# One scaling, two stores and a few pieces of bookkeeping change their steps at the end of the attention, before an MoE

## The chip, the core and the metric

The kernel runs on one core of a Trainium2 chip. A core has a matmul engine (TensorE, PE in the profile) and three engines for elementwise work: VectorE (DVE), ScalarE (ACT) and GpSimd (POOL). SyncE (SP) issues transfers between the chip's memory (HBM) and on-chip memory (SBUF); POOL issues the indirect ones. Matmuls write to PSUM, which DVE and ACT read. Each engine works off its instructions in the order of the program and waits for the others through semaphores. The metric is the time of one execution on the device, in microseconds.

## The reference

The inputs are q, k, v of shape (8, 12, 448, 64) in float32 (8 batches, 12 heads, 448 positions) and the weights of a mixture of 8 experts.

```
scores = cap * tanh(q @ k^T / 8 / cap)            # cap 30
attn   = softmax(scores)                          # over the keys
x      = (attn @ v) as rows of 768, 3584 tokens   # 12 heads side by side
e      = argmax(x @ w_gate);  g = softmax(x @ w_gate)[e]
out    = g * (relu(x @ w1[e]) @ w2[e])            # w1: 768x1024, w2: 1024x768
```

## The kernel before

**Attention.** The 12 heads of a batch are 6 pairs, so there are 48 pairs and a loop of 49 steps, n = 0 to 48. Step n computes the scores of pair n (`scores`, PE, then tanh and exp on ACT), the sums of exponentials of pair n in two additions on DVE and a third for the short last 64 keys (`adds`; POOL does the third, except for the last pair, where DVE does it), and the product with v of pair n - 1 (`pv`, PE), whose result DVE copies to a tile `ot`. `turn` transposes on DVE the `ot` of pair n - 2 into a tile `yt` that collects a batch.

**What follows a batch.** When batch b is through (step n = 6b + 6), a chain of small pieces is spread over the next steps: `rec_v`, `rec_p`, `rec_c` (reciprocals of the sums, DVE, PE, DVE), `logits` (PE, into PSUM tile ps_l), `log_v` (DVE, writes `lr`), `log_p` (PE, ps_l again), `route_v` (DVE), `route_s` (ACT), `place_p` (PE), `route_g` (DVE), `place_v` (DVE: reads ps_l and counts tokens of each expert), `scale` (DVE: two halves of `yt`, 128 x 1344 each, times gate and reciprocal), `store` (SP: four transfers of `yt` into `xd` in HBM, each of 32 partitions of both halves) and `place_d` (POOL: the tokens' numbers scattered to their slots in `ids`).

**Order.** The whole program is ordered by hand; each engine gets its instructions in the order in which the code below emits them. Pieces are put at a step and at one of six places in it by `at(step, place, function, ...)` (line 1033), and within a place they run in the order of the calls. Step n emits: `turn(n - 2)`; place 0; `scores(n)`, first half; `pv(n - 1)`, first half; place 5; `adds(n, 0)`; `scores(n)`, second half; place 3; `pv(n - 1)`, second half, with the copy to `ot`; place 6; `adds(n, 1)`; place 1; place 2. Step 48 has no scores: it begins with `adds(47, 1)`, and goes on with place 0, `pv(47)`, places 5, 3, 6, 1 and 2.

For batch 6 (the seventh) `log_v` stands in step 45, `place_p`, the second scaling and the first two stores in step 47, the last two stores in step 48. Batch 7's first `logits` stand in step 48, place 5.

**The first blocks of the experts.** Tokens are worked off in blocks of at most 448 of one expert. Block -1 is chosen after batch 4 and its rows are gathered from `xd` into `xg` during batches 5 and 6. Each of its 6 parts (128 of the 768 columns) is then transposed by DVE (`trans_x`, into one of three tiles `xt`), rounded by ACT to a high part (`high_x`) and subtracted by DVE to a low part (`low_x`); products use high and low parts of both factors, three matmuls for one. Block -2 is chosen by `first_block(1)`, 20 small DVE instructions in a row that `decide(k)` issues in pieces of k steps.

**After step 48** comes block -1: `up(-1, f)` (PE: 18 matmuls into one of two tiles ph; ACT: Relu to the high part of the hidden rows; DVE: the low part), and among it the pieces of batch 7 and the splits of weights into high and low. Behind `up(-1, 0)` stand on PE the last sums and `logits` of batch 7, `up(-1, 1)`, `rec_p(7)` and `up(-1, 2)`; on DVE, behind the low part of `up(-1, 0)`, stands `rec_v(7)`; on SP, behind the stores of step 48, the row of block -2's expert (`first_row`) and the loads of its weights (`load_w0`). The hidden rows of the first three f lie in `h0`, a tile that takes the name and the pool of the tiles `yt`, of which there are two buffers, given out in turn; batches 0, 2 and 4 use other memory:

```
 345               yts[b] = yp.tile([128, QB, XW], F32, name="yt", bufs=2)
 943       hb = h0 if j == -1 and f < 3 else m["hb"]
 945       A.activation(out=hh, in_=ph, func=AF.Relu)
 946       V.scalar_tensor_tensor(out=hl, in0=ph, scalar=0.0, in1=hh, op0=ALU.max, op1=ALU.subtract)
1147       h0 = yp.tile([128, QB, XW], F32, name="yt", bufs=2).rearrange("p q x -> p (q x)").bitcast(F32R)
1148       up(-1, 0)
1162       first_row(1)
1163       for f in range(2):
1164           load_w0(-2, f)
1165       rec_v(b)
```

Of the kernel before, what the change touches and what calls it, by code (L numbers as in the profile page):

```python
# [15 lines left out]
B, H, S, D = 8, 12, 448, 64  # L16
# [110 lines left out]
def attention_moe(tc, qT, kT, vL, capd, wgL, w1a, w1b, w2a, w2b, cst, cmk, out):  # L127
    nc = tc.nc
    V, A, G, PE = nc.vector, nc.scalar, nc.gpsimd, nc.tensor
# [903 lines left out]
    def at(step, when, f, *a):  # L1033
        tasks.setdefault((step, when), []).append((f, a))
# [5 lines left out]
    for b in range(B):  # L1040

        n = b * NP + NP
        for g in range(1, NP, 2):
            i = b * NP + g
            at(i + 2, 5, sums, i)
        at(n, 5, logits, b, range(4))
        at(n + 1, 3 if b == B - 1 else 5, logits, b, range(4, NP))
        if b == B - 1:
            break
        at(n + 1, 6, rec_v, b)  # L1050
        at(n + 2, 3, rec_p, b)
        at(n + 2, 6, rec_c, b)
        at(n + 3, 0, log_v, b)
        at(n + 3, 6, log_p, b)
        at(n + 3, 1, route_v, b)
        at(n + 4, 5, route_s, b)
        at(n + 5, 5, place_p, b)
        at(n + 4, 6, route_g, b)
        at(n + 4, 1, scale, b, 0, V)
        at(n + 5, 0, scale, b, 1, V)  # L1060
        at(n + 5, 2, store, b, range(0, 2))
        at(n + 5, 6, place_v, b)
        at(n + 6, 2, store, b, range(2, 4))
        if b < B - 2:
            for q in range(4):

                at(n + (5 if b == B_FIRST[0] - 1 else 11 if b == 4 else 7), 2, place_d, b, q)
# [11 lines left out]
        g += w  # L1079


    for n, k, late in ((8, 0, 0), (7, 1, 0), (6, 2, 0), (6, 3, 0), (6, 4, 1), (5, 5, 0)):
        at(n_pairs - n, 2, trans_x, -1, k)
        at(n_pairs - n + 1 + late, 5, high_x, -1, k)
        at(n_pairs - n + 1 + late, 1, low_x, -1, k, V)
# [6 lines left out]
        for _ in range(k):  # L1092
            next(second, 0)

    for n, k in ((6, 3), (4, 10), (2, 6)):
        at(n_pairs - n, 6, decide, k)
    at(n_pairs, 0, high, 1, 1)
    at(n_pairs, 6, decide, 100)
# [43 lines left out]
    b = B - 1  # L1142
# [102 lines left out]
    for k in range(XT):  # L1245
# [15 lines left out]
    late = [  # L1261
        [(2, 0), (2, 1), (1, 4), (2, 2), (1, 5), (2, 3)],
        [(1, 6), (2, 4), (1, 7), (2, 5)],
        [(2, 6), (2, 7)],
    ]
# [101 lines left out]
    def value(t, bound, why):  # L1367
        return nc.values_load(t, min_val=0, max_val=bound, skip_runtime_bounds_check_because=why)

    more = value(tab["more"][0:1, :], 1, "zero or one")  # L1370
    with tc.If(more > 0):
        for i, name in ((0, "large"), (1, "small")):
            cols = range(0, NL) if i == 0 else range(NL, NL + NS)
            cols = [c for c in cols if c not in ORDER]
            n = value(
                tab["nbi"][0:1, i : i + 1], (NL, NS)[i], f"the {name} blocks that hold a token, at most that many"
            )
# [75 lines left out]
```

## Time and profile before

| | |
|---|---|
| median of 3 runs | 850.56 us (849.16 to 852.16) |
| profiled execution | 851.22 us, its span 849.2 us |
| ACT, DVE, POOL busy | 57%, 66%, 54% of the span |
| mean granted clock of PE | 0.993 of full speed |
| HBM | 101.4 MB read, 22.4 MB written |

Times in the profile count from the start of the span. L505 is line 505 of the kernel. A row of the timeline gives start and length, and in brackets how long the engine had nothing to do before it and which instruction released it; lengths include the time for which an instruction stood issued but could not run. SPq and ACTq are instructions of a queue, such as issuing a transfer or taking a semaphore. Step 46 on DVE runs from about 342.7 to 349.1 us, step 47 to 355.6, step 48 to 359.5; PE is ahead of DVE by up to one step.

### The profile page before, as it was taken

The numbers are of one execution on the slowest core, as the hardware profiler recorded it, in microseconds if no ns is written. First come the engines' busy times: TensorE is split into PE (matmuls) and PEld (weight loads), VectorE is DVE, ScalarE is ACT, GpSimd is POOL, SyncE is SP. The second block draws the span as 40 slices with busy tenths as digits, with TensorE's granted clock in tenths as the row PEclk, the third lists the DMA queues.
The fourth block names the chain that finished last, engine by engine and source line by source line (L and its number), as shares of the span: only waits on it lengthen the run. The fifth ranks groups of instructions, "written<-read, shape, count | busy, mean of one in ns | idle before, by whom it ended". The sixth has DMA issues, their size and how long they took to land.

```text
span 849.2 us, 12136 instructions
## 1 busy us (share of the span) xinstructions
PE 828.1 (98%) x4492; PEld 555.1 (65%) x4492; DVE 557.9 (66%) x914; ACT 484.0 (57%) x573; POOL 458.3 (54%) x390
## 2 busy tenths in 40 slices
PE   8999999999999998899999999999999999999996
PEld 3223232323222322379999899999999999999996
DVE  2659898989988999977872934734636437437631
ACT  7999898989888997532442522423323323324420
POOL 1423353535557654347257777578477575655832
PEclk9999999999999999999999999999999999999998
DMA  5232545554566665348655362455431125534311
GB/s 199 90 114 83 175 86 176 86 173 88 135 210 211 217 172 136 70 136 186 103 177 212 120 263 86 158 194 175 160 111 53 34 66 186 192 120 150 148 34 69
DMA packets 46883, 117.96 MB, mean 139 GB/s; under 512 B 8241, under 2 KB 27091, under 8 KB 43744
## 3 DMA queue, kind: packets, MB, share of 16 engines
q1 hardware_dynamic: 30688, 57.01, 24.5%
q0 software_dynamic: 15840, 59.86, 20.0%
q8 instruction: 37, 0.61, 0.4%
q10 hardware_dynamic: 288, 0.23, 0.1%
q14 instruction: 30, 0.25, 0.1%
HBM read 101.40 MB, written 22.36 MB: 146 GB/s over the span
## 4 chain that ended last, share of the span: by engine, by line
PE 78%; DVE 11%; ACT 6%; issue 3%; POOL 1%; DMA 1%; POOLq 0%; DVEq 0%; ACTq 0%
PE ph L940 26%; PE y L970 20%; PE sp L253 10%; PE po L320 9%; DVE p L282 3%; PE y L978 2%; ACT pt L264 2%; PE po L309 2%; ACT pt L273 2%; PE ps_s L358 2%; PE sp L260 2%; PE ps_l L372 1%; PE po L970 1%; PE z L970 1%; DVE xl L917 1%
## 5 line engine op out<-in xcount | busy, mean ns | idle before, releaser
L290 POOL TENSOR_TENSOR p<-p,pr 64x896 f32<-64x896 f32 x47 | 106.4, 2264 | 182.7 <-DVE p L282 125.0
L945 ACT ACTIVATE hb<-ph 128x448 fp32r<-128x448 f32 (+1 forms) x69 | 35.1, 509 | 280.6 <-PE ph L940 176.2
L946 DVE SCALAR_TENSOR_TENSOR hb<-ph,hb 128x448 fp32r<-128x448 f32 (+1 forms) x69 | 39.8, 578 | 199.1 <-ACT hb L945 198.9
L802 POOL DMA_INDIRECT xg<-xd,xi x114 | 135.5, 1188 | 44.5 <-issue 29.5
L264 ACT ACTIVATE pt<-sp,qsc 128x896 f32<-128x896 f32 x144 | 139.3, 1001 | 25.2 <-PE sp L253 23.1
L253 PE MATMUL sp<-qr,kr 64*128 64x448 f32 x576 | 137.1, 580 | 3.2 <-ACT pr L264 1.6
L273 ACT ACTIVATE pt<-pt,capt 128x1792 f32<-128x1792 f32 x94 | 133.1, 1416 | 2.3
L320 PE MATMUL po<-pt,vr 128*64 128x448 f32 x576 | 130.0, 559 | 0.0
L812 POOL DMA_INDIRECT out<-ys,xi x98 | 108.5, 1107 | 29.3 <-issue 27.2
L253 PEld LDWEIGHTS sp<-qr,kr 64*128 64x128 f32 x576 | 47.7, 188 | 87.2 <-issue 43.6
L282 DVE TENSOR_TENSOR p<-pt 128x896 f32<-128x896 f32 x48 | 81.4, 1696 | 31.7 <-ACT pt L273 25.4
L320 PEld LDWEIGHTS po<-pt,vr 128*64 128x64 f32 x576 | 33.0, 136 | 82.2 <-issue 81.9
L282 DVE TENSOR_TENSOR p<-p,pt 128x896 f32<-128x896 f32 x48 | 53.0, 1103 | 15.6 <-ACT pt L273 14.7
L544 POOL DMA_INDIRECT ids<-tok,slots x32 | 37.0, 1158 | 9.9 <-issue 5.8
L913 ACT CAST xh<-xt 128x448 fp32r<-128x448 f32 (+1 forms) x54 | 27.2, 532 | 20.3 <-DVE xt L910 20.3
L802 POOL DMA_INDIRECT w1r<-in_w1b,widx x7 | 10.0, 1435 | 44.0 <-DVE w17l L848 43.7
L336 DVE COPY ot<-po 128x448 f32<-128x448 f32 x48 | 29.5, 614 | 5.9 <-PE po L320 5.7
L952 POOL COPY pace<-hb 128x1 f32<-128x1 f32 x52 | 17.3, 332 | 27.8 <-ACT hb L945 27.5
L910 DVE STREAM_TRANSPOSE xt<-xg 128x448 f32<-128x448 f32 (+1 forms) x54 | 30.2, 586 | 0.8
L917 DVE TENSOR_TENSOR xl<-xt,xh 128x448 fp32r<-128x448 f32 (+1 forms) x54 | 28.7, 560 | 0.0
L309 PE MATMUL po<-pr,vr 64*64 64x448 f32 x192 | 26.2, 562 | 0.0
L264 ACT ACTIVATE pr<-sp,qsc 128x896 f32<-128x896 f32 x24 | 23.9, 995 | 2.9 <-PE sp L260 2.9
(418 smaller groups left out, 1927.5 us busy)
## 6 DMA issues: line engine op xcount, KB each, us to landing
vr<-in_vL SPq DMA_DIRECT2D x24, 448.0 KB, 5.8
kr<-in_kT SPq DMA_DIRECT2D x23, 448.0 KB, 3.5
qr<-in_qT SPq DMA_DIRECT2D x23, 448.0 KB, 4.4
xd<-yt SPq DMA_DIRECT2D x20, 336.0 KB, 7.0
xd<-w2r SPq DMA_DIRECT2D x12, 336.0 KB, 7.1
w1r<-in_w1a SPq DMA_DIRECT2D x8, 384.0 KB, 5.4
w1r<-in_w1b SPq DMA_DIRECT2D x8, 384.0 KB, 6.4
w2r<-in_w2a SPq DMA_DIRECT2D x8, 384.0 KB, 6.2
```

The costliest lines, as they stand in the source:

```text
L253: PE.matmul(sp[:, j, 0:S], kr[r, i, c], qr[r, i, :], start=True, stop=True)
L264: A.activation(out=x, in_=sp[:, 0:2, 0:S], func=AF.Tanh, scale=qsc)
L273: A.activation(out=pt[:, lo:hi, :], in_=pt[:, lo:hi, :], func=AF.Exp, scale=capt)
L282: V.tensor_tensor(out=p4, in0=pt[:, 0:2] if half == 0 else p4, in1=pt[:, 2 * half + 2 : 2 * half + 4], op=ALU.add)
L290: e.tensor_tensor(out=p4[r], in0=p4[r], in1=rests[n // 2][r], op=ALU.add)
L309: PE.matmul(pvs[n + i][64 * j : 64 * j + 64, 0:S], vr[r, 12 + j, :], rests[n // 2][r, j], start=n + i > 0, stop=n + i == 0,)
L320: PE.matmul(po[64 * j : 64 * j + 64, 0:S], vr[:, n % 2 * 6 + 3 * j + t, :], pt[:, 2 * t + j], start=n == t == 0, stop=t == 2 and n > 0,)
L802: G.indirect_dma_start(out=dst, out_offset=None, in_=src, in_offset=bass.IndirectOffsetOnAxis(ap=idx.bitcast(U32), axis=0), bounds_check=b ...
L812: i = G.indirect_dma_start(out=dst, out_offset=bass.IndirectOffsetOnAxis(ap=idx.bitcast(U32), axis=0), in_=src, in_offset=None, bounds_che ...
L940: PE.matmul(ph, w[:, c], x[:, k, 0:n], start=i == 0, stop=i == 3 * KC - 1)
L946: V.scalar_tensor_tensor(out=hl, in0=ph, scalar=0.0, in1=hh, op0=ALU.max, op1=ALU.subtract)
L970: PE.matmul(y[k][:, 0:LARGE], w[:, c], h, start=f == 0 and i == 0, stop=f == FC - 1 and i == 2)
```

## The change

Three edits, all in the table of pieces; no instruction is new, and none goes.

```diff
-        at(n + 5, 0, scale, b, 1, V)
-        at(n + 5, 2, store, b, range(0, 2))
+        at(n + (5 if b < B - 2 else 6), 0 if b < B - 2 else 1, scale, b, 1, V)
+        at(n + (5 if b < B - 2 else 6), 2, store, b, range(0, 2))
...
-    for n, k, late in ((8, 0, 0), (7, 1, 0), (6, 2, 0), (6, 3, 0), (6, 4, 1), (5, 5, 0)):
+    for n, k, late in ((8, 0, 0), (8, 1, 0), (6, 2, 0), (6, 3, 0), (6, 4, 1), (4, 5, 1)):
         at(n_pairs - n, 2, trans_x, -1, k)
         at(n_pairs - n + 1 + late, 5, high_x, -1, k)
         at(n_pairs - n + 1 + late, 1, low_x, -1, k, V)
...
-    for n, k in ((6, 3), (4, 10), (2, 6)):
+    for n, k in ((6, 6), (4, 8), (2, 4)):
         at(n_pairs - n, 6, decide, k)
```

- Batch 6 alone (b = B - 2): its second scaling goes from step 47, place 0 (right behind `turn`) to step 48, place 1, behind both of `adds(47, 1)`, the copy to `ot` and place 6; its first two stores go from step 47, place 2 to step 48, place 2, where they stand ahead of the other two.
- Part 1 of block -1's rows: transpose from step 41 to 40, high and low from 42 to 41. Part 5: transpose from 43 to 44 (place 2 each), high (place 5) and low (place 1) from 44 to 46. In step 46 that low stands behind the first scaling of batch 6.
- `decide` issues 6, 8 and 4 steps of `first_block(1)` in steps 42, 44 and 46 where it issued 3, 10 and 6.

## Rows read from the trace of the kernel before

**Rows 1.** The page of the profiled execution: its first part (busy time, share of the span, instructions of each engine), the rate in 40 equal slices of the span, the group of the subtractions that make low parts of rows (busy time, mean ns), and the group of stores into `xd` out of tiles `yt` (count, size of one, median us to landing).
```profile
PE 828.1 (98%) x4492; PEld 555.1 (65%) x4492; DVE 557.9 (66%) x914; ACT 484.0 (57%) x573; POOL 458.3 (54%) x390
...
GB/s 199 90 114 83 175 86 176 86 173 88 135 210 211 217 172 136 70 136 186 103 177 212 120 263 86 158 194 175 160 111 53 34 66 186 192 120 150 148 34 69
...
L917 DVE TENSOR_TENSOR xl<-xt,xh 128x448 fp32r<-128x448 f32 (+1 forms) x54 | 28.7, 560 | 0.0
...
xd<-yt SPq DMA_DIRECT2D x20, 336.0 KB, 7.0
```

**Rows 2.** Who PE waited for in the stretch 280 to 372 us: the waiting instruction's tile and line, the one waited for, us in total, times, longest.
```profile
PE ps_l L372 <- DVE pos L533: 2.5, 1, 2.5
PE ps_l L446 <- DVE lr L441: 2.0, 1, 2.0
PE sp L253 <- ACT pr L264: 1.4, 1, 1.4
```

**Rows 3.** PE's instructions in order of time, neighbours of one kind merged (start us, us, engine, line, operation, out<-in, form, count, and in brackets the idle time before them with its releaser), around the end of the attention.
```profile
354.48 1.10 PE L372 MATMUL ps_l<-ot,wg 128*32 128x448 f32 x8 [2.52 <-DVE pos L533]
...
361.72 0.96 PE L358 MATMUL ps_s<-p,cs 128*32 128x448 f32 x8
...
367.09 0.47 PE L413 MATMUL ps_s<-rb,mk 128*128 128x42 bf16 x12
```

**Rows 4.** Busy time of the engines in three stretches (us): length, then PE, weight loads, DVE, ACT, POOL with their counts, the granted clock of PE as a share of full speed, DMA share, GB/s.
```profile
324.10:325.60 1.50, 0.14 (x4) 0.06 (x2) 1.50 (x3) 1.50 (x3) 0.00 (x0) 1.00 0.61 60
334.70:338.10 3.40, 3.35 (x10) 1.68 (x10) 3.40 (x3) 0.74 (x1) 1.55 (x1) 0.50 0.02 4
355.20:358.50 3.30, 3.30 (x12) 1.47 (x9) 3.23 (x5) 0.00 (x0) 0.00 (x0) 0.50 0.96 210
```

**Rows 5.** DVE's instructions in order of time, from step 46 to the start of the experts (columns as in rows 3).
```profile
345.68 0.15 DVE L604 TENSOR_TENSOR mx<-mx,k 128x1 f32<-128x1 f32 x1
...
347.58 1.55 DVE L505 TENSOR_TENSOR yt<-yt,rr 128x1344 f32<-128x1344 f32 x1
349.05 0.64 DVE L347 STREAM_TRANSPOSE yt<-ot 128x448 f32<-128x448 f32 x1
349.61 2.89 DVE L505 TENSOR_TENSOR yt<-yt,rr 128x1344 f32<-128x1344 f32 x1
352.43 1.08 DVE L282 TENSOR_TENSOR p<-pt 128x896 f32<-128x896 f32 x1
353.43 0.61 DVE L336 COPY ot<-po 128x448 f32<-128x448 f32 x1
...
354.77 0.95 DVE L848 TENSOR_TENSOR w10l<-w1r,w10h 128x768 fp32r<-128x768 f32 x1
355.64 1.09 DVE L282 TENSOR_TENSOR p<-p,pt 128x896 f32<-128x896 f32 x1
356.76 1.09 DVE L290 TENSOR_TENSOR p<-p,pr 64x896 f32<-64x896 f32 x1
357.88 0.62 DVE L336 COPY ot<-po 128x448 f32<-128x448 f32 x1
...
362.40 0.62 DVE L946 SCALAR_TENSOR_TENSOR yt<-ph,yt 128x448 fp32r<-128x448 f32 x1 [2.88 <-ACT yt L945]
...
364.99 0.18 DVE L403 CAST rb<-rec 128x42 bf16<-128x42 f32 x1
```

**Rows 6.** POOL's instructions in order of time: three of its additions of the short last rows of keys.
```profile
258.57 3.00 POOL L290 TENSOR_TENSOR p<-p,pr 64x896 f32<-64x896 f32 x1
...
340.12 2.10 POOL L290 TENSOR_TENSOR p<-p,pr 64x896 f32<-64x896 f32 x1 [3.87 <-DMA ids<-tok,slots]
347.81 3.28 POOL L290 TENSOR_TENSOR p<-p,pr 64x896 f32<-64x896 f32 x1 [5.59 <-PE ps_l L519]
```

**Rows 7.** DVE's instructions in order of time at four earlier places: beside POOL's addition at 258.57, the transpose of part 5, the end of `log_v(6)`, and beside POOL's addition at 340.12.
```profile
259.55 2.98 DVE L282 TENSOR_TENSOR p<-pt 128x896 f32<-128x896 f32 x1
...
323.35 0.64 DVE L910 STREAM_TRANSPOSE xt<-xg 128x448 f32<-128x448 f32 x1
...
333.76 0.94 DVE L441 TENSOR_REDUCE lr<-lt 128x112 f32<-128x448 f32 x1
...
340.18 2.17 DVE L471 TENSOR_TENSOR ohm<-tko,cs 128x112 f32<-128x112 f32 x1
```

**Rows 8.** The transfers that touch `xd`: of the stretch 354.5 to 356 (the last two stores of batch 6), and of 89 to 93 (the four of batch 0): line, queue, count, ns min/median/max of the issue, first and last start; and us from issue to landing.
```profile
L510 SPq DMA_DIRECT2D xd<-yt x2: 1352/1602/1852, 353.4 to 354.8; - x2
...
DMA to landing us min/median/max: 6.2/6.4/6.7
...
L510 SPq DMA_DIRECT2D xd<-w2r x4: 330/1052/1836, 89.5 to 92.0; - x4
...
DMA to landing us min/median/max: 5.9/6.3/6.8
```

**Rows 9.** The instructions of line 945 (the Relu of `up`) in the stretch 350 to 370: the waits that ACT's queue takes ahead of them, ns min/median/max, first and last start.
```profile
L945 ACTq EVENT_SEMAPHORE  x3: 17/38/38, 357.7 to 361.0; - x3
```

**Rows 10.** ACT's instructions in order of time: the high of part 5, the exponential of step 47's first half, and the first Relu of block -1.
```profile
324.02 0.57 ACT L913 CAST xh<-xt 128x448 fp32r<-128x448 f32 x1 [1.03 <-DVE xt L910]
...
347.81 1.79 ACT L273 ACTIVATE pt<-pt,capt 128x1792 f32<-128x1792 f32 x1
...
361.82 0.55 ACT L945 ACTIVATE yt<-ph 128x448 fp32r<-128x448 f32 x1 [9.41 <-PE ph L940]
```

## The prediction

> **What bounds the kernel now.** I read the page's first part, then TensorE's waits over the stretch that the change touches (280 to 372 us), then the timelines there, engine by engine, with the granted clock beside them. The first part shows the matmul engine PE busy for 98% of the span [rows 1]; whatever makes PE wait adds to the time, and so does a lower clock while it works. The waits name three places [rows 2]: 1.4 us in step 44 for a ScalarE (ACT) result, 2.0 us before `log_p(6)` in step 45, 2.5 us before `logits(7)` in step 48, the last two for VectorE (DVE). The timeline shows how PE goes on after them [rows 3]; the windows show what a wait costs besides: after the last two the granted clock is 0.50 of 2.4 GHz, that is 1.2 GHz, for 3.4 us, after the 1.4 us one it stays at full speed [rows 4]. While PE has work without a gap, 3.4 us at half speed cost 1.7 us.
>
> The last wait is the one that the change aims at. `place_v(6)` must read PSUM tile ps_l before `logits(7)` may write it. On DVE it stands behind the second scaling of batch 6 [rows 5]: that one lasts 2.89 us, against 1.55 for the first, since GpSimd's (POOL's) addition of step 46 runs until 347.81 + 3.28 = 351.09 us [rows 5, 6].
>
> **What the move takes away and puts in its place.** Out of step 47 goes the scaling; into step 46, right behind the first scaling, comes `low_x` of part 5, another subtraction with two SBUF inputs. `decide` issues one small instruction less there (L604, 0.15 us). POOL's addition has then been released and waits for the first scaling, and what DVE issues next with two inputs is held: at 258.57 POOL waited in the same way behind a scaling (its row is 3.00 long), and DVE's next addition stood from 259.55 to 262.53, which is 0.96 us beyond POOL's end and 0.1 less than the operation alone takes [rows 5 to 7]. So I put `low_x` (0.56 alone [rows 1]) at POOL's end, 351.09 - 0.15 = 350.94, plus 0.46: 351.40. Before, a transpose (0.56 from start to start) ran beside POOL in this time; now it comes after: 351.95. Then by the rows' starts the addition 1.00, copy and `place_v` 1.34: 354.3, where the row of before has 354.77 [rows 5]. `logits(7)` gains 0.5 us, not the 2.9 of the scaling. PE still idles for 2.52 - 0.5 = 2.0 us, as long as before `log_p(6)`, and I let the clock drop as it did there. The ends: nothing (`low_x` dearer than thought), and 1.1 + 1.7 us if `low_x` slips in ahead of POOL, because a wait of 1.4 us left the clock alone [rows 2, 4].
>
> **What the scaling and its stores meet in step 48.** From 354.3 DVE has, by the rows' starts, `low` of w10 0.87, the addition 1.12, the one that POOL does in other steps 1.12, and the copy of `ot` 0.62: 358.0. PE's last products for that copy, behind `logits(7)`, end near 356.8 and don't hold it. Then the scaling, without POOL beside it, 1.55: 359.5, against 349.61 + 2.89 = 352.50 before, which is 7.0 later [rows 5]. All four stores of the batch now wait for it, also the two that were issued in step 47, in the same SP burst: before, SP issued the four one behind the other from 352.53 on, and the last two, issued at 353.4 and 354.8, took 6.2 to 6.7 us [rows 8]. So the last lands near 361.0, 8.5 us after the first issue.
>
> What is late next is `h0`. It is the sixth tile named `yt` (after those of batches 1, 3, 5, 6 and 7) from a pool of two buffers, so it lies where batch 6's lay, and its first writer, ACT's Relu of `up(-1, 0)`, has to wait for all four stores. The trace has this wait: ACT's queue takes the events ahead of that instruction between 357.7 and 361.0, the last as the last store lands, and the instruction starts at 361.82, when PE's products are done [rows 9, 10]. The cover of before is 0.8 us. With the move the stores land at 359.5 + 8.5 = 368.0, while `up(-1, 0)` is done near 361.3 (half a microsecond before its old end at 361.8).
>
> Queued behind that Relu on ACT are the next high parts and Relus; behind its DVE half (start 362.40, 0.58 after ACT's) is `rec_v(7)`, whose last cast ends at 364.99 + 0.18 = 365.17 [rows 5]. PE's next instruction that needs it is `rec_p(7)`, behind `up(-1, 1)`, at 367.09 and without idle time [rows 3]. After: Relu 368.0, DVE half 368.6, last cast 371.35, `rec_p(7)` 371.4. PE is 4.3 us late, having stood for about 4.8. After a wait this long I take another drop at the price of the rows, 1.7 us, where the wait before `logits(7)` keeps its own. Of what follows PE has 0.2 us to give back (a small wait behind `up(-1, 2)`, which I see gone since DVE is only 4.3 late). **Sum: 4.3 + 1.7 - 0.2 = 5.8 us.**
>
> A burst like this one took as long elsewhere: four stores from 89.5 to 92.0 took 5.9 to 6.8 each, so the last landed 8.4 to 9.3 us after the first issue [rows 8]; upper end for the burst 9.3, that is +0.8. As lower end I take the four (336 KB each) at the best slice of the page, 263 GB/s: 1.376 MB in 5.2 us [rows 1]. I take 8.5, the same stores' own. The Trainium skill, "DMA: Bandwidth & Descriptors", section "Anatomy of one DMA", fits one DMA on the software path as about 2.0 us plus its bytes at 436 GB/s; as an estimate the four together would by that take 2.0 + 3.2 = 5.2 us, and the sum would be that of the first rival. The rows speak against it: 8.5 us for these very stores.
>
> **The other edits.** Part 1's transpose, high and low go one step earlier, part 5's transpose one later, and its high and low two later; `decide` takes 6, 8, 4 instead of 3, 10, 6 of its steps. On ACT the high of part 5 no longer stands in step 44, where it waited 1.03 us for its transpose (323.35 to 323.99) and kept `pr` waiting [rows 7, 10]: PE's 1.4 us there go. But PE then stands longer before `log_p(6)`, since `lr` comes from DVE at 333.76 + 0.94 [rows 7]. DVE has one low less ahead of it (part 5's, 0.56) and one small instruction of `decide` more, and the low of part 1 meets a POOL addition in step 41 as that of part 5 does in step 46, where a transpose ran beside it. I put `lr` 0.4 us earlier. That doesn't last: POOL's addition at 340.12 is released by the landing of id scatters, not by DVE, and holds DVE's L471 from 340.18 to 342.35 [rows 6, 7]. What steps 40 to 45 win or lose up to there is swallowed; so I count nothing. If that cover is gone, it is 1.7 less (no drop before `log_p(6)`) to 0.5 more. ACT pays 0.57 for the high of part 5 in step 46: the exponentials that DVE's addition of step 47 needs end at 349.60 + 0.57 = 350.2 at the latest, and that addition now starts at 351.95 [rows 10]. On SP only the expert loads of block -2 stand behind the stores; they come some 6 us later, and are first read behind `up(-1, 7)` (line 1243). Behind the scaling on DVE stand the memset for `load_ids(-2)`, whose gather on POOL comes about 1 us later and is read by `make_idx(-2)`, behind `log_v(7)`, and the low of w11, done near 360.5 and needed by `up(-1, 1)` near 363.5.
>
> The terms are of the profiled execution, 851.22 us with 2.0 us around its span; the median of the three runs is 0.7 lower. 850.6 + 5.8 = 856.4.
>
> **Rivals.**
> - *The stores bind, but little* (0.13): they drain in about 5.2 us with the queue to themselves, or the steps before bring DVE forward. Landing 364.7, cast 368.1, `rec_p(7)` 1.0 late, and a stand of 1.5 us, after which the clock stays. That is 1.0 - 0.2 = 0.8 us, or up to 3.4 where the clock drops after all or the stores take a microsecond more: 851.4 to 854. Against it: the two bursts of the rows.
> - *The write to `h0` is not held by the stores* (0.09, faster): the three events would belong to other waits, and the cover of `up(-1, 0)` lasts. Then only what `logits(7)` wins is left: 0.5 us, or 2.8 if the clock doesn't drop either: 847.8 to 850.1. It decides at ACT's first Relu: if that starts when PE's products end, near 361, this case holds. Against it: the last event at 361.0 falls on the landing.
> - *All is hidden* (0.05): `low_x` takes the scaling's place one to one, and what the stores cost is given back in the waits behind. 850.6, within 0.3%.
> - *Worse than the sum* (0.04): late stores and expert loads in one queue, two drops instead of one: 859 to 861.
>
> My forecast has 0.69, and by itself 854 to 858.8 (burst 7.5 to 9.3 us, the clock's price halved or half as much again, DVE 0.5 either way). The range for 8 in 10 takes in most of the first rival: 851.8 to 859.0. A difference within 0.3%, 2.6 us here, is about what a measurement can't tell from none. By the cases: slower by more 0.80, within 0.11 (half of the small binding among it), faster by more 0.09.
>
> **What would show it.** ACT's first Relu into `yt` starts at the last store's landing, 6 us later than before and well after PE's products; PE has a wait of 4 to 5 us before L413, named DVE or ACT, and the windows after it show 0.50; the wait at L372 is near 2.0; DVE's scaling lasts 1.55 at about 358, and `low_x` of part 5 some 2.5 at about 349. The wait at L253 in step 44 is gone. The forecast is wrong if L413 follows `up(-1, 1)` without a gap, or the Relu starts while stores are still under way.

## The result, and the profile after

The changed kernel takes 857.63 us (median of 6, 855.89 to 859.03), the kernel before 851.05 us in the same measurement: a ratio of 1.0062, 95% interval 1.0045 to 1.0079, so slower by some 5.3 us. The two medians by themselves lie 6.6 us apart, at the upper end of that interval. The profiled execution is the fastest of the six (span 853.9 us, 855.89 in all), and lies 4.7 us above the one of before. PE's busy time is that of before; in this execution the time went into waits.

```profile
PE 828.3 (97%) x4492; PEld 556.6 (65%) x4492; DVE 555.5 (65%) x914; ACT 483.2 (57%) x573; POOL 457.1 (54%) x390
```

PE's waits in the stretch 280 to 380 us of the changed kernel (tile and line, the one waited for, us in total, times, longest):

```profile
PE ps_s L413 <- DVE rb L403: 6.3, 3, 5.8
PE ps_l L372 <- DVE pos L533: 1.9, 1, 1.9
PE ps_l L446 <- DVE lr L441: 1.4, 1, 1.4
PE po L309 <- DVE ot L336: 0.5, 1, 0.5
PE sp L253 <- ACT pr L264: 0.2, 1, 0.2
```

Against [rows 2]: the wait at L253 is 0.2 instead of 1.4 us, those at L446 and L372 are 1.4 and 1.9 instead of 2.0 and 2.5. In their place stands a new one, 6.3 us at L413, `rec_p(7)`, called the stand below. In PE's timeline it lies behind `up(-1, 1)`, where [rows 3] have no gap, and is taken three times, once for each of the three casts that `rec_v(7)` makes:

```profile
351.89 0.96 PE L372 MATMUL ps_l<-ot,wg 128*32 128x448 f32 x8 [1.91 <-DVE pos L533]
...
357.51 0.96 PE L358 MATMUL ps_s<-p,cs 128*32 128x448 f32 x8
...
368.83 0.22 PE L413 MATMUL ps_s<-rb,mk 128*128 128x42 bf16 x1 [5.79 <-DVE rb L403]
369.29 0.19 PE L413 MATMUL ps_s<-rb,mk 128*128 128x42 bf16 x1 [0.23 <-DVE rb L403]
369.74 0.51 PE L413 MATMUL ps_s<-rb,mk 128*128 128x42 bf16 x10 [0.27 <-DVE rb L403]
...
380.94 0.18 PE L517 MATMUL ps_l<-ob,mk 128*128 128x40 bf16 x1 [0.67 <-DVE ob L480]
```

ACT's timeline names what held the chain, and the queue's row for line 945 and the row of the stores say the same. The first Relu has PE's products from about 357.5 on and starts at 366.35, released by the transfer of `yt`; the last event in ACT's queue comes at 366.3. The four stores were issued from 357.5 to 359.8:

```profile
366.35 0.54 ACT L945 ACTIVATE yt<-ph 128x448 fp32r<-128x448 f32 x1 [15.93 <-DMA xd<-yt]
```

```profile
L945 ACTq EVENT_SEMAPHORE  x3: 17/38/38, 362.8 to 366.3; - x3
```

```profile
L510 SPq DMA_DIRECT2D xd<-yt x4: 330/912/1892, 357.5 to 359.8; - x4
...
DMA to landing us min/median/max: 3.3/5.3/6.4
```

On DVE the part 5 low is held beside POOL's addition (2.50 us, 0.62 alone), the scaling runs alone in 1.56 and ends at 357.50, DVE's half of the hidden rows (L946) waits 8.55 us for ACT's, and the last cast of `rec_v(7)` ends at 369.69:

```profile
346.88 2.50 DVE L917 TENSOR_TENSOR xl<-xt,xh 128x448 fp32r<-128x448 f32 x1
...
355.94 1.56 DVE L505 TENSOR_TENSOR yt<-yt,rr 128x1344 f32<-128x1344 f32 x1
...
366.93 0.62 DVE L946 SCALAR_TENSOR_TENSOR yt<-ph,yt 128x448 fp32r<-128x448 f32 x1 [8.55 <-ACT yt L945]
...
369.51 0.18 DVE L403 CAST rb<-rec 128x42 bf16<-128x42 f32 x1
```

The granted clock in four stretches (columns as in [rows 4]): behind the wait at L372 it stays at full speed (2.4 GHz); PE's last product ahead of the stand ends at 363.0, the clock is still full until 365.1, then falls to 1.2 GHz, and stays there until 375.3:

```profile
352.00:355.30 3.30, 3.30 (x20) 1.76 (x18) 3.20 (x6) 0.00 (x0) 0.00 (x0) 1.00 0.02 5
363.10:365.10 2.00, 0.00 (x0) 0.00 (x0) 0.00 (x0) 0.00 (x0) 0.00 (x0) 1.00 0.94 195
365.20:368.80 3.60, 0.00 (x0) 0.00 (x0) 1.78 (x4) 2.43 (x4) 0.00 (x0) 0.50 0.75 232
368.90:375.30 6.40, 5.90 (x26) 5.15 (x27) 5.84 (x13) 0.00 (x0) 0.96 (x1) 0.50 0.22 64
```

### The profile page after: what moved, and what is told of

It is laid out like the page before. It is cut to its first block, busy times and chain, and to the rows that moved or that the text cites. A ratio compares the mean times of both kernels' runs of the same rounds, so it can differ in the third digit from the quotient of the medians.

```text
span 853.9 us, 12138 instructions
## 1 busy us (share of the span) xinstructions
PE 828.3 (97%) x4492; PEld 556.6 (65%) x4492; DVE 555.5 (65%) x914; ACT 483.2 (57%) x573; POOL 457.1 (54%) x390
## 4 chain that ended last, share of the span: by engine, by line
PE 79%; DVE 9%; ACT 4%; issue 4%; POOL 2%; DMA 1%; SPq 0%; POOLq 0%; DVEq 0%; ACTq 0%
PE ph L940 24%; PE y L970 19%; PE sp L253 11%; PE po L320 10%; PE y L978 2%; DVE p L282 2%; PE po L309 2%; PE sp L260 2%; PE ps_s L358 2%; ACT pt L264 2%; PE ps_l L372 1%; PE po L970 1%; PE z L970 1%; ACT pt L273 1%; DVE xl L917 1%
## 5 line engine op out<-in xcount | busy, mean ns | idle before, releaser
L946 DVE SCALAR_TENSOR_TENSOR hb<-ph,hb 128x448 fp32r<-128x448 f32 (+1 forms) x69 | 39.7, 577 | 199.0 <-ACT hb L945 198.8
L253 PE MATMUL sp<-qr,kr 64*128 64x448 f32 x576 | 135.5, 574 | 1.9 <-ACT pt L264 1.3
L253 PEld LDWEIGHTS sp<-qr,kr 64*128 64x128 f32 x576 | 47.2, 186 | 84.9 <-issue 44.3
L282 DVE TENSOR_TENSOR p<-pt 128x896 f32<-128x896 f32 x48 | 77.9, 1622 | 31.6 <-ACT pt L273 25.4
L802 POOL DMA_INDIRECT w1r<-in_w1b,widx x7 | 10.0, 1433 | 44.6 <-DVE w17l L848 44.3
L917 DVE TENSOR_TENSOR xl<-xt,xh 128x448 fp32r<-128x448 f32 (+1 forms) x54 | 32.5, 629 | 0.0
```

What stands on the lines that cost most here:

```text
L253: PE.matmul(sp[:, j, 0:S], kr[r, i, c], qr[r, i, :], start=True, stop=True)
L282: V.tensor_tensor(out=p4, in0=pt[:, 0:2] if half == 0 else p4, in1=pt[:, 2 * half + 2 : 2 * half + 4], op=ALU.add)
L802: G.indirect_dma_start(out=dst, out_offset=None, in_=src, in_offset=bass.IndirectOffsetOnAxis(ap=idx.bitcast(U32), axis=0), bounds_check=b ...
L917: e.tensor_tensor(out=m["xl"][:, k, 0:n], in0=xts.pop((j, k)), in1=m["xh"][:, k, 0:n], op=ALU.subtract)
```

## The experiments

Ratios are to the kernel before on the same chip, with 95% intervals. The chips differ: the kernel before has medians of 851.05, 856.88, 854.11 and 856.14 us in the four measurements, so only ratios, or runs of one measurement, are set against each other.

**First edit alone** (scaling and stores of batch 6; the rest as before).

```diff
-    for n, k, late in ((8, 0, 0), (8, 1, 0), (6, 2, 0), (6, 3, 0), (6, 4, 1), (4, 5, 1)):
+    for n, k, late in ((8, 0, 0), (7, 1, 0), (6, 2, 0), (6, 3, 0), (6, 4, 1), (5, 5, 0)):
...
-    for n, k in ((6, 6), (4, 8), (2, 4)):
+    for n, k in ((6, 3), (4, 10), (2, 6)):
```

> The first edit alone: batch 6's second scaling and first two stores in step 48, parts and decide as before. Theory (the stores behind the late scaling hold the Relu into h0): the scaling ends near 358.7 us, the last store lands 8.5 later near 367.2, L413 starts near 370.6 after a stand of 5 to 6.5 us, the clock falls for 6 to 10 us: 857 to 859, slower than before by about 7. Rival (the shifted parts and decide cost the time, the moved scaling only frees place_v): 847 to 849, and L413 follows up(-1, 1) without a gap.

Measured: 1.0052 [1.0027, 1.0078]. PE's waits from 300 to 390 us:

```profile
PE ps_s L413 <- DVE rb L403: 6.1, 3, 5.6
PE ps_l L446 <- DVE lr L441: 2.3, 1, 2.3
PE ps_l L372 <- DVE pos L533: 2.2, 1, 2.2
```

The stand before L413 is there without the other two edits, and so is the loss: some 4.5 us by the ratio, where about 7 had been expected.

**Second and third edit alone.**

```diff
-        at(n + (5 if b < B - 2 else 6), 0 if b < B - 2 else 1, scale, b, 1, V)
-        at(n + (5 if b < B - 2 else 6), 2, store, b, range(0, 2))
+        at(n + 5, 0, scale, b, 1, V)
+        at(n + 5, 2, store, b, range(0, 2))
```

> The second and third edit alone: parts and decide as in the changed kernel, scaling and stores of batch 6 as before. Theory: steps 44 and 45 are brought forward by about 2 us without a fall of the clock at L446; in step 47 DVE has the low of part 5 and the scaling ahead of place_v, so PE waits about 3.3 us at L372 and its clock falls there; the stores land near 360 and don't hold the Relu. 849 to 850.5, that is 0 to 2 us faster than before. Rival (the parts cost the time): 855 or more.

Measured: 1.0008 [0.9980, 1.0036], no difference that can be told. The gain that I expected (up to 2 us) isn't there. Its source was an advance of steps 44 and 45, and the profile shows none: from `log_p(5)` to `log_p(6)` it is 46.4 us, as in the profile of the kernel before. What was expected behind that came about: the held low and the scaling stand one behind the other ahead of `place_v(6)`, PE waits 3.9 us for it (3.3 expected), longer than before, and L413 follows without a gap:

```profile
348.62 1.55 DVE L505 TENSOR_TENSOR yt<-yt,rr 128x1344 f32<-128x1344 f32 x1
350.09 2.52 DVE L917 TENSOR_TENSOR xl<-xt,xh 128x448 fp32r<-128x448 f32 x1
...
353.10 1.51 DVE L505 TENSOR_TENSOR yt<-yt,rr 128x1344 f32<-128x1344 f32 x1
```

```profile
356.59 1.72 PE L372 MATMUL ps_l<-ot,wg 128*32 128x448 f32 x8 [3.94 <-DVE pos L533]
...
369.25 0.47 PE L413 MATMUL ps_s<-rb,mk 128*128 128x42 bf16 x12
```

**`h0` a tile of its own, in the changed kernel.** The edit takes away what makes the Relu wait: `h0` no longer lies in the buffer of batch 6's `yt`.

```diff
-    h0 = yp.tile([128, QB, XW], F32, name="yt", bufs=2).rearrange("p q x -> p (q x)").bitcast(F32R)
+    h0 = yp.tile([128, QB, XW], F32, name="h0").rearrange("p q x -> p (q x)").bitcast(F32R)
```

> The changed kernel, but h0 is a tile of its own and not the buffer of batch 6's yt: nothing is left out. Theory: the Relu starts when PE's products end, near 357.5, rec_v(7) is through near 361.2, L413 follows up(-1, 1) at 363.0 without a gap and at full clock: 4.1 us earlier than before, 846.5 to 847.5. Rival 1 (the delay of the stores and of the expert loads behind them on SP costs the time, whoever writes h0): 855 or more, with the waits of PE at weights' splits. Rival 2 (the clock is the cost, by the gaps before step 48): 853 to 856.

Measured: 0.9975 [0.9949, 1.0000], a gain of some 2 us on the kernel before, half of what was expected; neither rival's loss is there. Since the changed kernel had been measured on another chip, both were run once more side by side:

> The changed kernel itself once more, on one chip with the next run, so that the two can be set against one kernel before. Theory: 1.004 to 1.008 of the kernel before, as in its first measurement; L413 stands 5 to 6.5 us. Rival (the first measurement held chance of that chip): within 0.3% of the kernel before.

> The changed kernel with h0 a tile of its own once more, beside the changed kernel. Theory: 0.996 to 1.000 of the kernel before, so 5 to 9 us below the changed kernel on the same chip; L413 follows up(-1, 1) without a gap. Rival: less than 3 us apart.

Measured: the changed kernel 1.0067 [1.0044, 1.0090], 861.31 us; with `h0` of its own 0.9973 [0.9947, 1.0000], 853.77 us. They are 7.5 us apart (the two profiled executions 5.1, since later parts differ too). This pair of profiles is the clearest view of the mechanism, since both reach `logits(7)` at the same time. PE and ACT of the changed kernel:

```profile
354.54 0.96 PE L372 MATMUL ps_l<-ot,wg 128*32 128x448 f32 x8 [1.91 <-DVE pos L533]
...
371.50 0.22 PE L413 MATMUL ps_s<-rb,mk 128*128 128x42 bf16 x1 [4.21 <-DVE rb L403]
```

```profile
369.01 0.54 ACT L945 ACTIVATE yt<-ph 128x448 fp32r<-128x448 f32 x1 [15.93 <-DMA xd<-yt]
```

And with `h0` of its own:

```profile
354.52 0.96 PE L372 MATMUL ps_l<-ot,wg 128*32 128x448 f32 x8 [2.55 <-DVE pos L533]
...
367.17 0.47 PE L413 MATMUL ps_s<-rb,mk 128*128 128x42 bf16 x12
```

```profile
361.83 0.54 ACT L945 ACTIVATE h<-ph 128x448 fp32r<-128x448 f32 x1 [9.07 <-PE ph L940]
```

The Relu starts 7.2 us earlier, L413 stands right behind `up(-1, 1)` and 4.3 us earlier. The stores are as late in one as in the other (the scaling starts at 358.6 in both), so late stores and the expert loads behind them on SP cost nothing by themselves that can be told. It is the write to `h0` that makes them cost. The stand is 4.2 us here, under the 5 to 6.5 expected: in this execution the clock fell behind L372, and PE came to L413 later. From the start of `logits(7)` to L413 it is the same as in the first profile: 371.50 - 354.54 = 16.96 us here and 368.83 - 351.89 = 16.94 there, set by the landing and not by PE.

**The same edit in the kernel before.**

> The kernel before, with h0 a tile of its own: the wait that the change makes late is taken away where it had a cover of 0.8 us. Theory: no difference, 850.5 to 851.5; the Relu starts at PE's end, near 361.8. Rival (the wait already cost something before): 849 or less.

Measured: 0.9987 [0.9962, 1.0012]; the Relu starts at 361.45, when PE's products end. Before the change the shared buffer cost nothing that can be told. This run also bounds what the change gains once `h0` has its own tile: on the same chip the changed kernel with that tile is at 0.9975 and the kernel before with it at 0.9987, intervals that overlap, so a gain of the change itself isn't shown.

**The first edit alone, with `h0` of its own.**

> The first edit alone, and h0 a tile of its own. Theory: the Relu starts at PE's end, L413 follows up(-1, 1) without a gap; of the first edit only its gain is left, the wait at L372 falls to 1.2 to 2.2 us: 1 to 3 us faster than before. Rival (the late stores cost by the queue of SP): 3 us or more slower.

Measured: 0.9981 [0.9965, 0.9997]. The loss is gone, and the time lies a little below the kernel before; whether the move or the tile gives that, the ratio of 0.9987 for the tile alone leaves open. A shorter wait it is not: in its profile PE waits 2.6 us at L372, as long as before. `logits(7)` does come earlier, 17.9 us behind `log_p(6)` where the two profiles without any edit to the steps have 19.7 and 18.8, but PE is there earlier too.

**Scaling and stores in step 47 behind `place_v`**, in the changed kernel, `h0` in the old buffer.

```diff
-        at(n + (5 if b < B - 2 else 6), 0 if b < B - 2 else 1, scale, b, 1, V)
-        at(n + (5 if b < B - 2 else 6), 2, store, b, range(0, 2))
+        at(n + 5, 0 if b < B - 2 else 1, scale, b, 1, V)
+        at(n + 5, 2, store, b, range(0, 2))
```

> The changed kernel, but the second scaling of batch 6 and its stores in step 47 behind place_v (place 1) instead of step 48; h0 still in the old buffer. Theory (PE waits for the landing of the stores through h0): the scaling ends 3.0 to 3.7 us earlier against the start of logits(7), the landing and the Relu come earlier by the same, and the stand before L413 shrinks from 5.8 us to about 2.5; the time lies 3 to 5 us below the changed kernel, 0 to +3 us against the kernel before. Rival (what costs is that the scaling stands somewhere else than in step 47, place 0, or the shifted parts): no shrinking, 6 us slower as before.

Measured: 1.0017 [0.9990, 1.0043], no difference from the kernel before that can be told. PE and ACT:

```profile
356.99 0.96 PE L372 MATMUL ps_l<-ot,wg 128*32 128x448 f32 x8 [1.01 <-DVE pos L533]
...
369.95 0.19 PE L413 MATMUL ps_s<-rb,mk 128*128 128x42 bf16 x1 [1.23 <-DVE rb L403]
```

```profile
367.47 0.55 ACT L945 ACTIVATE yt<-ph 128x448 fp32r<-128x448 f32 x1 [11.05 <-DMA xd<-yt]
```

From the start of `logits(7)` to that of the Relu it is 10.5 us, against 14.5 in the changed kernel (351.89 to 366.35); the stand is 1.2 us (1.8 with its pieces) instead of 5.8 and 4.2 in the two profiles of the changed kernel; about 2.5 had been expected. The cost follows the landing of the stores.

**`rec_v(7)` and the split of w12 ahead of the first Relu**, in the changed kernel, `h0` in the old buffer. `up` is cut in two, so that its Relu and DVE half can stand later.

```diff
-    up(-1, 0)
+    up(-1, 0, False)
...
     split(1, 2)
+    relu(-1, 0)
     up(-1, 1)
```

> The changed kernel, h0 in the old buffer, but rec_v(7) and the split of w12 stand ahead of the first Relu and its DVE half on ACT and DVE. Theory (what stops PE first is not h0 but what is queued behind it): L413 follows up(-1, 1) without a gap; PE then waits at the first matmul of up(-1, 2) for the tile ph of up(-1, 0), until the stores have landed plus 1.2 us, some 4 us; up(-1, 2) starts about 2.5 us earlier than in the changed kernel and the time lies 2 to 4 us below it. Rival (the wait on h0 itself is the whole cost): no gain.

Measured: 1.0037 [1.0021, 1.0053]. L413 has no wait, and PE stands 4.0 us at the next place, the first matmul of `up(-1, 2)` (here line 942), until DVE's half of the hidden rows (here line 954) has read the tile ph:

```profile
367.86 0.47 PE L413 MATMUL ps_s<-rb,mk 128*128 128x42 bf16 x12
372.32 0.47 PE L942 MATMUL ph<-xh,w12h 128*128 128x448 f32 x1 [3.99 <-DVE yt L954]
```

So PE never waits for `h0` itself: first for `rec_v(7)`, queued behind the late write on DVE, and where that is out of the way, for the tile of two that the late write has not yet freed. How much time the order gives back, the two ratios of different chips (1.0062 and 1.0037, intervals that touch) don't settle. In the profiles `log_p(7)` starts 20.8 us after `logits(7)`, against 24.3 in the first profile of the changed kernel, both with full clock behind L372, so 3.5 us less in these two executions.

**`h0` of its own, and the low of part 5 behind `place_v`**, on top of the changed kernel.

```diff
-        at(n_pairs - n + 1 + late, 1, low_x, -1, k, V)
+        at(n_pairs - 1 if k == 5 else n_pairs - n + 1 + late, 1, low_x, -1, k, V)
```

> The changed kernel with h0 a tile of its own, and the low of part 5 in step 47 behind place_v, ahead of the low of w10, instead of step 46 behind the first scaling. Theory (that low meets POOL's addition and is held for 2 us): the low takes 0.6 us, the addition of step 47 is held in its place until POOL's end plus 0.95; place_v comes 0.5 to 1 us earlier, the wait at L372 falls by that, and where it falls under about 1.5 us the clock stays: 0.5 to 2.5 us below the run with h0 of its own alone, 3 to 5 us below the kernel before. Rival (POOL's addition is the pin, whatever stands behind it): the same as that run.

Measured: 0.9959 [0.9941, 0.9977], 850.25 us beside 854.11 for the kernel before: faster than both kernels. Against `h0` of its own alone (0.9975 and 0.9973) the intervals overlap, so what the place of the low adds isn't shown. DVE and PE:

```profile
352.28 1.21 DVE L282 TENSOR_TENSOR p<-pt 128x896 f32<-128x896 f32 x1 [1.14 <-ACT pt L273]
...
354.75 0.62 DVE L917 TENSOR_TENSOR xl<-xt,xh 128x448 fp32r<-128x448 f32 x1
```

```profile
354.47 0.96 PE L372 MATMUL ps_l<-ot,wg 128*32 128x448 f32 x8
...
365.54 0.47 PE L413 MATMUL ps_s<-rb,mk 128*128 128x42 bf16 x12
```

The low takes 0.62 us, the addition of step 47 is no longer held by POOL but waits for ACT, and `logits(7)` follows PE's products without a gap. But that is because PE came later, as in this profile its clock was low behind L446 (0.50 from 336.1 to 339.5): L533, the instruction of `place_v(6)` that L372 waits for, starts 18.2 us behind `log_p(6)`, against 18.1 with `h0` of its own alone, so that the low's new place didn't bring it forward here. Nor is the expectation's limit of 1.5 us for the clock borne out: waits of 1.8 us (the kernel before with `h0` of its own) and 2.2 us (the first edit alone) at L372 were followed by full clock.

## Why the prediction was right

**The forecast held**: slower, 856.4 us foretold, 857.63 measured, by the mechanism named. Step by step, against the working:

- *The low of part 5 takes the scaling's place and is held until POOL's end plus 0.46.* Right: 346.88 + 2.50 = 349.38 in the first profile, POOL's addition ends at 345.63 + 3.26 = 348.89 (the last row; the other two are for the last point of this list):

```profile
323.43 2.82 POOL L290 TENSOR_TENSOR p<-p,pr 64x896 f32<-64x896 f32 x1 [6.65 <-DVE yt L347]
...
338.15 2.09 POOL L290 TENSOR_TENSOR p<-p,pr 64x896 f32<-64x896 f32 x1 [3.86 <-DMA ids<-tok,slots]
345.63 3.26 POOL L290 TENSOR_TENSOR p<-p,pr 64x896 f32<-64x896 f32 x1 [5.39 <-DVE p L282]
```

- *`logits(7)` gains 0.5 us.* Not settled. From L446 (`log_p(6)`) to L372 it was 354.48 - 334.75 = 19.7 us before, and 19.1 and 19.0 in the two profiles of the changed kernel. But the kernel before with `h0` of its own, which has the same order up to there, took 18.8:

```profile
336.88 0.47 PE L446 MATMUL ps_l<-lr,cs 128*128 128x112 f32 x2 [2.25 <-DVE lr L441]
...
355.65 0.96 PE L372 MATMUL ps_l<-ot,wg 128*32 128x448 f32 x8 [1.78 <-DVE pos L533]
```

  That the clock drops at this place was right in one of the two profiles of the changed kernel: after the same wait of 1.91 us it stayed at full speed in the first, and fell for 3.4 us in the second:

```profile
356.00:359.30 3.30, 3.30 (x11) 2.37 (x8) 3.20 (x4) 0.00 (x0) 0.00 (x0) 0.50 0.02 5
369.60:376.40 6.80, 4.40 (x22) 3.84 (x23) 6.51 (x15) 1.84 (x3) 0.00 (x0) 0.50 0.35 114
```

- *The scaling 7.0 us later, the last landing 8.5 us after the first issue.* Right: the scaling ends 5.6 us after the start of `logits(7)` (5.5 foretold, 359.5 - 354.0), the last store lands 8.8 us after the first issue at 357.5. The estimate by the Trainium skill's fit ("DMA: Bandwidth & Descriptors", "Anatomy of one DMA") was 5.2 us. That fit is for one transfer on the software path; these are four in a row, issued by SP, and for them the 8.8 measured decides.
- *The Relu at the landing, `rec_p(7)` 4.3 us late.* Right: the pair on one chip has L413 at 371.50 and 367.17, 4.3 us apart. The stand itself was put at 4.8 us, and was 5.8 in one profile and 4.2 in the other, since it also depends on how early PE comes. The 4.3 holds against executions in which the clock falls behind L372, as in the profile of before (12.6 us from `logits(7)` to L413). In the kernel before with `h0` of its own the clock stayed up and it is 11.1 us, against which 5.9 us are lost. How often each kernel has the fall, the single profiles don't tell.
- *1.7 us for one fall of the clock.* Somewhat undersized. The low stretch behind the stand is 6.8 us in the second profile and 10.2 in the first, part of it spent in the stand. From L413 to the start of `up(-1, 3)` it is 6.8 us with the stand and 4.6 without in the pair (371.50 to 378.31, 367.17 to 371.80), so 2.2 us. About 0.5 us of that are the gaps between L413's pieces, which the sum didn't have, and 0.2 us of idle time at L446 are gone, which leaves some 1.9 for the clock. The same working for the first profile, against that of before, gives 2.6.
- *0.2 us given back.* It comes to about nothing: the small wait behind `up(-1, 2)` is gone, but a new one of 0.67 (0.55 in the second profile) stands at L517, where `place_p(7)` waits for DVE, and takes it back.
- *Steps 40 to 45 count nothing, `lr` 0.4 us earlier.* About right for the time (the two edits alone: 1.0008). From `log_p(5)` to `log_p(6)` it is 44.6 to 48.6 us with them in eight profiles, 46.4 to 47.7 without in four, so chance moves it as much as the edits do. The cover that I named did give way in the first profile: POOL's addition of step 45 came 2.0 us earlier, at 338.15, since the id scatters that release it were issued after an addition that came at 323.43 instead of 326.29, as in this row of before:

```profile
326.29 2.09 POOL L290 TENSOR_TENSOR p<-p,pr 64x896 f32<-64x896 f32 x1 [8.56 <-DVE rr L419]
```

  That and the clock that stayed up behind L372 fit a profiled execution that is the fastest of its six.

The sum was 5.8 us; the ratios 1.0062 and 1.0067 make it 5.3 and 5.7, the medians 6.6 and 5.2. The mechanism and its largest term, 4.3, are shown. That the whole agrees so closely is in part luck: the gaps at L413 and the longer fall of the clock add some 0.7 to 1.4 us that weren't in the sum, and what the change wins or loses ahead of `logits(7)` varies by more than that between executions. The rival that the write to `h0` isn't held by the stores fell with the first profile, and that late stores cost by themselves with the pair.

## What to carry to other kernels

When an instruction is put later, look up who writes next into the memory that its readers still hold: here a store that nobody waits for was the last reader of a buffer that a later tile gets by rotation, and 0.8 us of cover was all that hid it. Here the price was not paid by the writer but by what is queued behind it on its engines, and then again by the matmul clock. A tile of its own cost nothing that can be told (0.9987 in the kernel before) and took the loss away (1.0067 to 0.9973 on one chip); that the change is then a gain beyond the tile's own isn't shown.

## What the runs showed that I had not expected

The same wait of 1.91 us ahead of `logits(7)` was followed by full clock in one execution of the changed kernel and by 3.4 us at half in another. From L372 to L358, behind `up(-1, 0)`, it took 5.6 us in the one and 7.2 in the other, so such a fall, at 1.6 us, may hide the effect of a small edit in single executions. In the changed kernel this fall cost nothing at L413, since it only shortened the stand. And in the first profile the clock fell 2 us after PE had run dry, and was still at half for 6.5 us after PE had taken up work again.
